# Moving a range's half products into the next range's w_in stage

## The chip, the cores and the metric

One core of a Trainium2 chip runs the whole kernel. The metric is the time of one execution on the device in microseconds; the median of three executions stands for a kernel.

## What is computed

Attention of 12 heads over 8 batches of 448 tokens, then two matrix products with a leaky ReLU between them:

```
attn = softmax(q @ k^T / sqrt(64)) @ v            # q, k, v: 8 x 12 x 448 x 64
x = attn, heads side by side                      # 3584 x 768
h = x @ w_in                                      # 768 x 2048
out = max(0.01 * h, h) @ w_out                    # 2048 x 768
```

The inputs are float32; the kernel's matmuls take bfloat16 and add up in float32.

## The kernel before

**Ranges.** The 3584 tokens are cut into seven ranges, numbered 0 to 6 here (`cuts`): 640, 512, 512, 512, 512, 384 and 512 tokens. From range 1 on, a range i has two stages. `hidden(i)` is its w_in stage: h from x. `second(i)` is its w_out stage: out from h. Attention work for later ranges is put between the matmuls of both.

**The w_in stage** (`hidden`). Matrix products are done in a form with seven products where eight would be plain (sums and differences of blocks are made on VectorE first, so that one product in eight is saved). A group of four 128-wide row blocks of h takes seven products of six matmuls each (L553), 256 token columns wide (192 in range 5). Two groups run in turn, one on the PSUM tiles `banks` (named g in the profile) and one on two of the three `slots` (named sc), and there are two such rounds: 28 products. After a product ScalarE copies it (L565, L573, L577) or VectorE adds it to such a copy (L568, L580, L583); ScalarE writes the leaky ReLU (L542). The sums and differences of h that w_out needs are L525 and L526, those of x that w_in needs are L500 (`mix_x_part`, eight for a range: four over two row blocks and four over one), with six copies L487 at range 2, where the ring that holds x begins anew.

**The w_out stage** (`second`). It walks through two pairs of 128-token blocks (`block_pair(i, c)`, c = 0 and 1). A pair has six products of eight 128x384 matmuls (L682), in turn on the banks b and a; the names `fifth` and `sixth` are the last two of them. Between matmuls, at every `yield`, `second` may put in scores of later attention units (L316, L319; their exponentials are L328 on ScalarE) or `rows`, the weighted sums over v (L340, L347) with their division on VectorE (L968, L969). Scores take all three slots at once, rows and the last part of a unit's scores one. A finished row block is transposed into x by a DMA of the SP queue (L271), q and k of later units into qkT likewise (L280). `keep` (L687) copies a product into the output tile, `join` (L693) adds one, `store` (L399) sends it out; L697 and L703 are differences of h for the pair.

**The half products** (`deep`). What would be the seventh product of both pairs is done together, by the same scheme once more: seven products of four 128x192 matmuls (L644). Each is followed by an addition into an output tile (L645); one more difference of h is L647, and three others are made ahead in `deep_sums` (L620). The seven lie among the fifth and sixth product of the second pair, one after every two matmuls, and use two slots, b and a, alternately; they come in the order b, a, b, a, b, a, b. While they run, only one slot is left for attention work. In the last range, the kernel's end, they stand in the same places; its second pair has its output tiles in the memory of the exponentials (named e).

**What sets the order.** The program fixes the order on each engine; an engine works through its instructions one after the other and waits where a semaphore tells it to. In `second(i)`, the subtractions L500 of the next range are put in one at a time as steps go by, once the planner's clock says that x has arrived; those left over are put at the end of the stage, ahead of `hidden(i + 1)`. In `hidden(i)`, `rows` is called at steps 2, 6, 10, ... as long as rows are owed; two are.

**Tiles.** A slot is one tile of 128 x 2 x 512 float32 numbers. There are three output tiles `o`, five tiles `c` for the copies of w_in products.

```
banks = [ps_g.tile([P, 4 * P], F32, name=f"g{i}") for i in range(2)]
slots = [ps_s.tile([P, 2, 512], F32, name=f"sc{i}") for i in range(3)]
```

Of the kernel before, what the change touches and what calls it, by code (L numbers as in the profile page):

```python
# [16 lines left out]
def kernel(  # L17
# [9 lines left out]
    nc = tc.nc  # L27

    B, H, S, D = q.shape
    DM, DF = moe_w_in.shape  # L30
# [497 lines left out]
    def hidden(i):  # L528

        n = cuts[i + 1] - cuts[i]  # L530
        nh = n // 2
        at = place_of(cuts[i])
        near, far = slice(0, KH), slice(KH, KD)
        one, two = slice(at, at + nh), slice(at + nh, at + n)
        t2, t3, t4 = (x_mix[:, x, :, :nh] for x in range(3))
        hs = h[:, :, spots(i)[0] * P:spots(i)[0] * P + n]
        taken = [next_slot() for _ in range(2)]
        del slots[1:]
        chains = [banks, [x[:, 0] for x in taken]]

        def act(m, cols, x):
            nc.scalar.activation(  # L542
                hs[:, m:m + 2, cols], x.rearrange("p (m t) -> p m t", m=2), AX.Prelu, alpha=0.01
            )

        def group(chain, m):
            b, a = (x[:, :2 * nh] for x in chain)
            left, right = slice(0, nh), slice(nh, n)

            def product(ps, w, x, first=False):  # L550
                for j in range(2):
                    for kk in range(KH):
                        nc.tensor.matmul(  # L553
                            ps[:, j * nh:(j + 1) * nh], w[:, kk, ts(j, P)], x[:, kk],
                            start=(first and j == 0 and kk == 0), stop=(kk == KH - 1), skip_group_check=True,
                        )

            def fresh():
                return c_pool.tile([P, 4 * P], F32, name="c")[:, :2 * nh]

            cl, ch = slice(m * P, (m + 2) * P), slice(FH + m * P, FH + (m + 2) * P)
            s2, s3, s4 = (w_in_mix[:, x, :, cl] for x in range(3))
            product(b, w_in_sb[:, near, cl], xT[:, near, one], first=True)
            c11 = fresh()
            nc.scalar.copy(c11, b)  # L565
            yield
            product(a, w_in_sb[:, far, cl], xT[:, far, one], first=True)
            nc.vector.tensor_add(c11, c11, a)  # L568
            yield
            product(b, s2, t2)  # L570
            act(m, left, c11)
            c12 = fresh()
            nc.scalar.copy(c12, b)  # L573
            yield
            product(a, w_in_sb[:, near, ch], xT[:, near, two], first=True)
            c22 = fresh()
            nc.scalar.copy(c22, a)  # L577
            yield
            product(b, s3, t3)
            nc.vector.tensor_add(c22, c22, b)  # L580
            yield
            product(a, s4, xT[:, far, two])
            nc.vector.tensor_add(c12, c12, a)  # L583
            act(MH + m, right, c22)
            yield
            product(b, w_in_sb[:, far, ch], t4)
            act(m, right, c12)
            act(MH + m, left, b)
            yield

        ready = []
        for r in range(2):
            ms = [4 * r, 4 * r + 2]
            todo = [group(chains[x], ms[x]) for x in range(2)]
            for step in range(7):
                for x in range(2):
                    yield
                    next(todo[x])
                    if step == 2 and ready:
                        mix_h(i, ready.pop(0))  # L600
            for c in chains:
                c.reverse()
            ready += ms
        slots.extend(taken)
        for m in ready:
            mix_h(i, m)
# [16 lines left out]
    def deep(i):  # L623

        one, two = (ts(x[1], P) for x in spots(i)[1])
        lo, hi = slice(MH, MH + QH), slice(MH + QH, MD)
        s3, s1 = h_mix[:, :QH, 0], h_mix[:, QH:, 0]
        t, (t2, t3, t4) = w_mix[:, 2], (deep_mix[:, x] for x in range(3))
        left, right = slice(0, QW), slice(QW, NW)
        o = [kept[i, c] for c in range(2)]  # L630
        end = i + 1 == NR
        taken = [slots.pop(0) for _ in range(2)]
        b, a = (x[:, 0, :QW] for x in taken)
        for ps, first, x, w, c, cols in (
            (b, True, h[:, lo, one], t[:, :QH, left], 0, left),
            (a, True, h[:, hi, one], t[:, QH:, left], 0, left),
            (b, False, s1, t2, 0, right),
            (a, True, h[:, lo, two], t[:, :QH, right], 1, right),
            (b, False, s3, t3, 1, right),
            (a, False, h[:, hi, one], t[:, QH:, right], 0, right),  # L640
            (b, False, h[:, hi, two], t4, 1, left),
        ):
            for m in range(QH):
                nc.tensor.matmul(ps, x[:, m], w[:, m], start=(first and m == 0), stop=(m == QH - 1), skip_group_check=True)  # L644
            nc.vector.tensor_add(o[c][:, cols], o[c][:, cols], ps)  # L645
            if ps is a and first and c == 0:
                nc.vector.tensor_sub(h[:, hi, one], h[:, hi, one], s1)  # L647
            t0 = token(i, spots(i)[1][c][1])
            if ps is a and not first:
                store(o[0], t0, slice(0, NW) if end else slice(0, DM), (nc.sync, nc.scalar if end else nc.sync))  # L650
            if end and c == 1 and ps is b:
                store(o[1], t0, cols, (nc.sync, nc.scalar))
            yield
        if not end:
            store(o[1], token(i, spots(i)[1][1][1]))
        slots.extend(taken)
        for x in taken:
            model["free"][id(x)] = model["now"] + 1.2

    def block_pair(i, c):  # L660

# [30 lines left out]
        def join(o, at, ps):  # L692
            nc.vector.tensor_add(o[:, at], o[:, at], ps[:, :NW])  # L693

        yield
        yield from product(b, h[:, lo, one], w_out_sb[:, lo, left], first=True)
        nc.vector.tensor_sub(h[:, lo, one], h[:, lo, two], h[:, lo, one])  # L697
        short = cuts[i + 1] - cuts[i] < 4 * P
        keep(o1, left, b, idle if c == 0 and short else calm)
        yield  # L700
        yield from product(a, h[:, hi, one], w_out_sb[:, hi, left], first=True)
        join(o1, left, a)
        nc.vector.tensor_sub(h[:, hi, one], h[:, hi, one], h[:, lo, one])  # L703
        yield
        yield from product(b, h[:, lo, one], t2)
        keep(o1, right, b, calm)
        yield
        yield from product(a, h[:, lo, two], t1, first=True)
        keep(o2, right, a, calm)
        yield  # L710

        def fifth():
            yield from product(b, s3, t3)
            if i:
                keep(o2, left, b)
            join(o2, right, b)
            if i:
                if last:
                    store(o1, token(i, x1), left)
                    store(o2, t0, right, (nc.sync, nc.scalar))  # L720
                elif i + 1 == NR:
                    store(o2, t0, right)

        def sixth():
            yield from product(a, h[:, hi, one], w_out_sb[:, hi, right])
            join(o1, right, a)
            store(o1, token(i, x1), right if last else slice(0, DM), (nc.sync, nc.scalar if last else nc.sync))

        if i and c:
            more = deep(i)  # L730
            for _ in fifth():
                yield
                next(more)
                yield
            yield
            for x, _ in enumerate(sixth()):
                yield
                if x != int(last):
                    next(more)
                    yield  # L740
            for _ in more:
                yield
            return
        yield from fifth()
        yield
        sums = deep_sums(i) if i else ()
        for _ in sixth():
            next(sums, None) if i else None
            yield
        if i:  # L750
            return
        yield
# [434 lines left out]
    for i in range(1, NR):  # L1187
        for step, _ in enumerate(hidden(i)):
            advance()
            if owed_t and step == 0:  # L1190
                tail()
            if step % 4 == 2 and rows_done < nxt:
                rows()
            turn_next(i)
        model.update(now=0.0, act=2.3, free={id(x): 0.9 if cuts[i + 1] - cuts[i] == 4 * P and i + 1 < NR else 1.2 for x in slots}, ready={})
        second(i)
# [30 lines left out]
```

## Time and profile before

| | us |
|---|---|
| median of 3 executions | 384.94 (384.92 to 384.98) |
| the profiled execution | 384.23 |
| its span in the profile | 382.4 |
| TensorE busy in it (granted clock 0.997) | 371.8 |
| VectorE, ScalarE, GpSimd busy | 247.6, 257.3, 182.2 |
| TensorE, w_in stage of range 2 (153.2 to 173.6) | 20.16 of 20.40 |
| TensorE, w_out stage of range 2 (173.6 to 201.4) | 27.75 of 27.80 |
| TensorE, end of the kernel (359.0 to 382.4) | 18.39 of 23.40 |

The span runs from the first to the last event of the execution that the profiler recorded. A timeline line names its start, its length, the engine, the line of the kernel, what is written and read, and in brackets how long the engine had been idle and what ended that. A line "x8" stands for eight instructions in a row; their length is that of the row. Matmuls overlap: the next one starts before the one before it has drained, so the distance of two starts says what a product costs.

### The profile page before, as it was taken

The numbers are of one execution on the slowest core, as the hardware profiler recorded it, in microseconds if no ns is written. First come the engines' busy times: TensorE is split into PE (matmuls) and PEld (weight loads), VectorE is DVE, ScalarE is ACT, GpSimd is POOL, SyncE is SP. The second block draws the span as 40 slices with busy tenths as digits, with TensorE's granted clock in tenths as the row PEclk, the third lists the DMA queues.
The fourth block names the chain that finished last, engine by engine and source line by source line (L and its number), as shares of the span: only waits on it lengthen the run. The fifth ranks groups of instructions, "written<-read, shape, count | busy, mean of one in ns | idle before, by whom it ended". The sixth has DMA issues, their size and how long they took to land.

```text
span 382.4 us, 10102 instructions
## 1 busy us (share of the span) xinstructions
PE 371.8 (97%) x4008; PEld 265.4 (69%) x4008; DVE 247.6 (65%) x551; ACT 257.3 (67%) x396; POOL 182.2 (48%) x376
## 2 busy tenths in 40 slices
PE   7999999999999999999999999999999999999994
PEld 3665557766698566886568866688666995678753
DVE  5763858356766867666676675775757774784744
ACT  6988885765768784488764788648786388518620
POOL 8998631987979554840558405685046100000000
PEclk9999999999999999999999999999999999999998
DMA  9999999799999569891499914999238700222032
GB/s 160 200 201 203 178 179 195 94 176 208 143 193 124 82 123 164 183 127 27 97 143 214 144 27 81 153 214 135 41 67 151 175 15 5 74 73 66 1 84 83
DMA packets 99456, 47.85 MB, mean 125 GB/s; under 512 B 63696, under 2 KB 96208, under 8 KB 99408
## 3 DMA queue, kind: packets, MB, share of 16 engines
q0 software_dynamic: 40384, 22.47, 47.6%
q1 hardware_dynamic: 58432, 24.12, 32.4%
q8 instruction: 31, 0.51, 0.5%
q10 hardware_dynamic: 592, 0.61, 0.5%
q14 instruction: 17, 0.14, 0.1%
HBM read 45.61 MB, written 11.01 MB: 148 GB/s over the span
## 4 chain that ended last, share of the span: by engine, by line
PE 89%; DVE 5%; issue 2%; DMA 1%; ACT 1%; POOL 0%; DVEq 0%; POOLq 0%; ACTq 0%
PE g L682 25%; PE g L553 14%; PE sc L553 14%; PE sc L319 7%; PE sc L347 6%; PE g L421 4%; PE sc L316 4%; PE sc L359 3%; PE g L769 3%; PE sc L644 2%; PE g L810 2%; PE sc L340 2%; DMA w_in_mix<-in_q_dram 1%; PE g L359 1%; PE g L298 1%
## 5 line engine op out<-in xcount | busy, mean ns | idle before, releaser
L328 ACT ACTIVATE e<-sc 128x896 bf16<-128x896 f32 (+1 forms) x144 | 123.6, 922 | 33.5 <-PE sc L319 20.4
L682 PE MATMUL g<-w_out_sb,h 128*128 128x384 bf16 x416 | 81.7, 326 | 0.2 <-DVE o L693 0.2
L682 PEld LDWEIGHTS <-h 128*128 128x128 bf16 x528 | 49.1, 98 | 37.5 <-issue 9.6
L186 POOL COPY qkb<-fq 112x512 bf16<-112x512 bf16 x36 | 23.7, 659 | 88.9 <-DMA qkT<-qkb 72.7
L542 ACT ACTIVATE h<-c 128x512 bf16<-128x512 f32 (+1 forms) x72 | 43.5, 611 | 24.8 <-DVE c L568 15.5
L553 PEld LDWEIGHTS <-w_in_sb 128*128 128x128 bf16 x576 | 54.3, 98 | 5.3
L553 PEld LDWEIGHTS <-w_in_mix 128*128 128x128 bf16 x432 | 41.2, 98 | 4.1
L968 DVE RECIPROCAL rec<-sc 112x8 f32<-112x8 f32 x42 | 8.7, 208 | 43.5 <-PE sc L347 22.0
L687 DVE COPY o<-g 128x384 f32<-128x384 f32 x44 | 24.3, 553 | 18.8 <-PE g L682 18.6
L347 PE MATMUL sc<-v,e 128*128 128x65 bf16 x720 | 33.3, 193 | 0.0
L319 PE MATMUL sc<-qkT 64*128 64x448 bf16 (+1 forms) x210 | 32.8, 352 | 0.0
L347 PEld LDWEIGHTS <-e 128*128 128x128 bf16 x720 | 31.2, 98 | 1.3
L969 DVE TENSOR_TENSOR x<-sc,rec 112x512 bf16<-112x512 f32 x42 | 29.0, 691 | 1.5
L553 PE MATMUL sc<-xT,w_in_sb 128*128 128x256 bf16 (+1 forms) x216 | 28.5, 268 | 0.0
L553 PE MATMUL g<-xT,w_in_sb 128*128 128x256 bf16 (+1 forms) x216 | 28.5, 268 | 0.0
L565 ACT COPY c<-g 128x512 f32<-128x512 f32 (+1 forms) x12 | 6.8, 569 | 32.0 <-PE g L553 32.0
L340 PE MATMUL sc<-v,e 128*128 128x130 bf16 x120 | 26.5, 221 | 0.0
L693 DVE TENSOR_TENSOR o<-o,g 128x384 f32<-128x384 f32 x36 | 19.7, 548 | 5.4 <-PE g L682 4.8
L682 PE MATMUL g<-w_mix,hmix 128*128 128x384 bf16 x104 | 23.0, 327 | 0.0
L159 POOL DMA_DIRECT2D fv<-in_v_dram x33 | 20.6, 631 | 4.1 <-POOL v L199 2.4
L159 POOL DMA_DIRECT2D fk<-in_k_dram x33 | 20.9, 645 | 1.4 <-DMA fv<-in_v_dram 1.4
L359 PEld LDWEIGHTS <-e 112*128 112x128 bf16 x432 | 20.0, 98 | 2.1 <-issue 0.7
(144 smaller groups left out, 745.4 us busy)
## 6 DMA issues: line engine op xcount, KB each, us to landing
fq<-in_q_dram POOLq DMA_DIRECT2D x18, 224.0 KB, 6.2
w_in_sb<-in_moe_w_in_dram POOLq DMA_DIRECT2D x4, 768.0 KB, 11.0
w_out_sb<-in_moe_w_out_dram POOLq DMA_DIRECT2D x4, 768.0 KB, 18.8
out_dram<-o SPq DMA_DIRECT2D x7, 336.0 KB, 3.2
out_dram<-o SPq DMA_DIRECT2D x7, 288.0 KB, 5.0
fk<-in_k_dram POOLq DMA_DIRECT2D x15, 128.0 KB, 6.3
fv<-in_v_dram POOLq DMA_DIRECT2D x15, 128.0 KB, 5.6
out_dram<-o SPq DMA_DIRECT2D x7, 240.0 KB, 3.4
```

What stands on the lines that cost most here:

```text
L159: nc.gpsimd.dma_start(out=t[p, :n, :, :so].rearrange("p u h so d -> p (u h) (so d)"), in_=(q, k, v)[x][b, hs, keys].rearrange("h (p so) d ...
L186: by(t[:SC, x].rearrange("p so h d -> p h so d"), f)
L319: nc.tensor.matmul(ps[:, j, :S].rearrange("p (so s) -> p so s", so=NSC), t[p, 1, c], t[p, 0, :, :SC], start=True, stop=True,)
L328: nc.scalar.activation(e[:, :, c, :], ps[:n, :, :S], AX.Exp, scale=scale)
L340: nc.tensor.matmul(ps, e[:, EM + qc * SC:EM + qc * SC + P], vt[:, 2 * KC:].rearrange("p j d -> p (j d)"), start=True, stop=False, skip_gro ...
L347: nc.tensor.matmul(ps[:, j * (D + 1):(j + 1) * (D + 1)], e[:, at:at + P], vt[:, j * KC + c], start=False, stop=(c == KC - 1), skip_group_c ...
L359: nc.tensor.matmul(ps[:, qc, :], t[:SC, at:at + P], vt[:, c], start=(c == 0), stop=(c == NSC - 1),)
L542: nc.scalar.activation(hs[:, m:m + 2, cols], x.rearrange("p (m t) -> p m t", m=2), AX.Prelu, alpha=0.01)
L553: nc.tensor.matmul(ps[:, j * nh:(j + 1) * nh], w[:, kk, ts(j, P)], x[:, kk], start=(first and j == 0 and kk == 0), stop=(kk == KH - 1), sk ...
L682: nc.tensor.matmul(ps[:, cols], x[:, m], w[:, m], start=(first and m == 0), stop=(m == MH - 1), skip_group_check=True,)
L687: by(o[:, at], ps[:, :NW])
L969: nc.vector.tensor_mul(x, ps[:, :, :, :D], rec.to_broadcast([SC, 2, 2 * NP, D]))
```

## The change

From range 2 on, `hidden(i)` runs the half products of range i - 1: one behind each of its first seven products. (Range 0 has none; those of range 6 have no w_in stage after them.) `deep` takes one slot and uses the tile's two halves as b and a. The w_out stage of ranges 1 to 5 ends with the fifth and sixth product alone. In `hidden(i)` from range 2 on, rows are called from step 10 on, no longer at steps 2 and 6.

In the last range the half products follow the second pair's second, third and fourth product, one after every four matmuls, and the seventh after the fourth product. Since its second output tile has no sum yet then, two of them are copied there by ScalarE (L649) instead of added, and the fifth product is added on its left side too. The sixth product is split into two halves of 192 columns, the first on bank a, the second on half a slot; the right part of the fourth product in bank a that is no longer added to is added by itself (L714), and each half is stored by itself. One store of the first output tile comes earlier.

```diff
@@ -589,6 +589,7 @@
             yield
 
         ready = []
+        more = deep(i - 1) if i > 1 else None
         for r in range(2):
             ms = [4 * r, 4 * r + 2]
             todo = [group(chains[x], ms[x]) for x in range(2)]
@@ -596,6 +597,8 @@
                 for x in range(2):
                     yield
                     next(todo[x])
+                    if i > 1:
+                        next(more, None)
                     if step == 2 and ready:
                         mix_h(i, ready.pop(0))
             for c in chains:
@@ -629,8 +632,8 @@
         left, right = slice(0, QW), slice(QW, NW)
         o = [kept[i, c] for c in range(2)]
         end = i + 1 == NR
-        taken = [slots.pop(0) for _ in range(2)]
-        b, a = (x[:, 0, :QW] for x in taken)
+        slot = slots.pop(0)
+        b, a = (slot[:, x, :QW] for x in range(2))
         for ps, first, x, w, c, cols in (
             (b, True, h[:, lo, one], t[:, :QH, left], 0, left),
             (a, True, h[:, hi, one], t[:, QH:, left], 0, left),
@@ -642,20 +645,18 @@
         ):
             for m in range(QH):
                 nc.tensor.matmul(ps, x[:, m], w[:, m], start=(first and m == 0), stop=(m == QH - 1), skip_group_check=True)
-            nc.vector.tensor_add(o[c][:, cols], o[c][:, cols], ps)
+            if end and c and (ps is a or cols is left):
+                nc.scalar.copy(o[c][:, cols], ps)
+            else:
+                nc.vector.tensor_add(o[c][:, cols], o[c][:, cols], ps)
             if ps is a and first and c == 0:
                 nc.vector.tensor_sub(h[:, hi, one], h[:, hi, one], s1)
-            t0 = token(i, spots(i)[1][c][1])
             if ps is a and not first:
-                store(o[0], t0, slice(0, NW) if end else slice(0, DM), (nc.sync, nc.scalar if end else nc.sync))
-            if end and c == 1 and ps is b:
-                store(o[1], t0, cols, (nc.sync, nc.scalar))
+                store(o[0], token(i, spots(i)[1][0][1]), slice(0, NW) if end else slice(0, DM))
             yield
         if not end:
             store(o[1], token(i, spots(i)[1][1][1]))
-        slots.extend(taken)
-        for x in taken:
-            model["free"][id(x)] = model["now"] + 1.2
+        slots.append(slot)
 
     def block_pair(i, c):
 
@@ -692,61 +693,73 @@
         def join(o, at, ps):
             nc.vector.tensor_add(o[:, at], o[:, at], ps[:, :NW])
 
-        yield
-        yield from product(b, h[:, lo, one], w_out_sb[:, lo, left], first=True)
-        nc.vector.tensor_sub(h[:, lo, one], h[:, lo, two], h[:, lo, one])
-        short = cuts[i + 1] - cuts[i] < 4 * P
-        keep(o1, left, b, idle if c == 0 and short else calm)
-        yield
-        yield from product(a, h[:, hi, one], w_out_sb[:, hi, left], first=True)
-        join(o1, left, a)
-        nc.vector.tensor_sub(h[:, hi, one], h[:, hi, one], h[:, lo, one])
-        yield
-        yield from product(b, h[:, lo, one], t2)
-        keep(o1, right, b, calm)
-        yield
-        yield from product(a, h[:, lo, two], t1, first=True)
-        keep(o2, right, a, calm)
-        yield
-
-        def fifth():
+        def early():
+            yield from product(b, h[:, lo, one], w_out_sb[:, lo, left], first=True)
+            nc.vector.tensor_sub(h[:, lo, one], h[:, lo, two], h[:, lo, one])
+            short = cuts[i + 1] - cuts[i] < 4 * P
+            keep(o1, left, b, idle if c == 0 and short else calm)
+            yield
+            yield from product(a, h[:, hi, one], w_out_sb[:, hi, left], first=True)
+            join(o1, left, a)
+            if last:
+                store(o1, token(i, x1), left)
+            nc.vector.tensor_sub(h[:, hi, one], h[:, hi, one], h[:, lo, one])
+            yield
+            yield from product(b, h[:, lo, one], t2)
+            keep(o1, right, b, calm)
+            yield
+            yield from product(a, h[:, lo, two], t1, first=True)
+            keep(o2, right, a, calm)
+            if last:
+                nc.vector.tensor_add(o1[:, NW + QW:], o1[:, NW + QW:], a[:, QW:NW])
+            yield
+
+        def late():
             yield from product(b, s3, t3)
-            if i:
+            if i and not last:
                 keep(o2, left, b)
             join(o2, right, b)
-            if i:
-                if last:
-                    store(o1, token(i, x1), left)
-                    store(o2, t0, right, (nc.sync, nc.scalar))
-                elif i + 1 == NR:
-                    store(o2, t0, right)
-
-        def sixth():
-            yield from product(a, h[:, hi, one], w_out_sb[:, hi, right])
-            join(o1, right, a)
-            store(o1, token(i, x1), right if last else slice(0, DM), (nc.sync, nc.scalar if last else nc.sync))
-
-        if i and c:
+            if last:
+                store(o2, t0, right, (nc.sync, nc.scalar))
+                join(o2, left, b)
+                store(o2, t0, left, (nc.sync, nc.scalar))
+            elif i + 1 == NR:
+                store(o2, t0, right)
+            yield
+            if not last:
+                yield from product(a, h[:, hi, one], w_out_sb[:, hi, right])
+                join(o1, right, a)
+                store(o1, token(i, x1))
+                return
+            for x, ps in enumerate((a, slots[0][:, 0])):
+                cols = ts(x, QW)
+                yield from product(ps, h[:, hi, one], w_out_sb[:, hi, right][:, :, cols], first=bool(x), cols=cols)
+                at = slice(NW + x * QW, NW + (x + 1) * QW)
+                nc.vector.tensor_add(o1[:, at], o1[:, at], ps[:, cols])
+                store(o1, token(i, x1), at, (nc.sync, nc.scalar))
+                if not x:
+                    yield
+
+        yield
+        if last:
             more = deep(i)
-            for _ in fifth():
+            for x, _ in enumerate(early()):
                 yield
-                next(more)
-                yield
-            yield
-            for x, _ in enumerate(sixth()):
-                yield
-                if x != int(last):
-                    next(more)
+                if x > 3 and x % 2:
+                    next(more, None)
                     yield
             for _ in more:
                 yield
+            yield from late()
             return
-        yield from fifth()
-        yield
-        sums = deep_sums(i) if i else ()
-        for _ in sixth():
-            next(sums, None) if i else None
-            yield
+        yield from early()
+        sums = deep_sums(i) if i and not c else iter(())
+        for x, _ in enumerate(late()):
+            if x > 3:
+                next(sums, None)
+            yield
+        for _ in sums:
+            pass
         if i:
             return
         yield
@@ -1189,7 +1202,7 @@
             advance()
             if owed_t and step == 0:
                 tail()
-            if step % 4 == 2 and rows_done < nxt:
+            if step % 4 == 2 and rows_done < nxt and (step > 8 or i == 1):
                 rows()
             turn_next(i)
         model.update(now=0.0, act=2.3, free={id(x): 0.9 if cuts[i + 1] - cuts[i] == 4 * P and i + 1 < NR else 1.2 for x in slots}, ready={})
```

## The prediction

> **What bounds the kernel now.** I read the page first, then the timeline of TensorE alone to list its gaps, then the timeline of all engines where w_out of one range ends and w_in of the next begins, then the last 15 us.
>
> ```profile
> PE 371.8 (97%) x4008; PEld 265.4 (69%) x4008; DVE 247.6 (65%) x551; ACT 257.3 (67%) x396; POOL 182.2 (48%) x376
> ```
>
> TensorE is busy for 371.8 of 382.4 us. The missing 10.6 us are 1.20 before the first matmul, some 3.2 in gaps of 0.13 to 0.44 up to 58 us, 1.07 + 0.12 at the ends of w_out stages, 0.23 in the last stage, and 4.8 behind the last matmul. From 58 us to 377 us TensorE rarely waits, so any wait put there is paid in full, and the most that can be won in the middle is about 1.4 us. The 1.07 us are these two waits in range 1:
>
> ```profile
> 152.57 0.49 PE L644 MATMUL sc<-w_mix,h 128*128 128x192 bf16 x4 [0.69 <-DVE o L645]
> ...
> 153.44 0.49 PE L644 MATMUL sc<-deep_mix,h 128*128 128x192 bf16 x4 [0.38 <-DVE o L645]
> ```
>
> A half product waits there for VectorE to have added up the one two places earlier. In range 2 the same place shows 0.06 us:
>
> ```profile
> 196.94 0.49 PE L682 MATMUL g<-w_mix,hmix 128*128 128x384 bf16 x2
> 197.14 0.56 DVE L687 COPY o<-g 128x384 f32<-128x384 f32 x1 [1.71 <-PE g L682]
> 197.61 0.41 DVE L500 TENSOR_TENSOR x_mix<-xT 128x512 bf16<-128x512 bf16 x1
> ...
> 201.41 0.49 PE L644 MATMUL sc<-w_mix,h 128*128 128x192 bf16 x4
> 201.73 0.29 DVE L500 TENSOR_TENSOR x_mix<-xT 128x256 bf16<-128x256 bf16 x1
> ...
> 202.19 0.82 PE L553 MATMUL g<-xT,w_in_sb 128*128 128x256 bf16 x6
> 202.84 0.82 PE L553 MATMUL sc<-xT,w_in_sb 128*128 128x256 bf16 x6
> ```
>
> The reader is to see three things. A product of six w_in matmuls takes 0.655 us (202.19 to 202.84). VectorE starts 0.20 us after TensorE has passed on (the fifth product begins at 196.94, the copy of the fourth at 197.14). And the token subtractions of the next range (L500) stand between the additions, in a queue that works in order.
>
> **The prices.** Eight 128x384 matmuls take 1.30 us (368.64 to 369.94), four 128x192 ones 0.33. On VectorE, counted to the next start: copy and addition of 384 columns 0.47 and 0.46, addition of 192 columns (L645) 0.27, or 0.35 to its end; subtraction L500 of 512 columns 0.33, or 0.46 where it needs the one just before (0.42 + 0.04); of 256 columns 0.33 in a dependent row (342.01, 342.33, 342.66, 342.99); addition L568 0.60; L653, the old L647, 0.33. TensorE goes on 0.06 after the end of an addition (152.17 + 0.34 to 152.57).
>
> **The moved half products.** Their 5 x 28 matmuls and 35 additions are the same work in another place: 0 on TensorE as long as no wait comes. In the changed kernel's order of instructions one comes. Both halves now lie in one tile, and each half product waits for the addition of the half product just before it, where it waited for the one two before. One round is 0.20 + 0.35 + 0.06 = 0.61 us, and the cover is one w_in product, 0.655: enough, if VectorE is free at once. It is not. All subtractions L500 of the next range now stand ahead of the first of these additions, because w_out's two last products are 2.3 us (7 x 0.33) shorter and nothing separates them from the stage's end.
>
> Range 2 to 3, counted from the fifth product's start F. VectorE: copy to 0.67, two L500 to 1.43, copy of the fifth product from 1.50, addition to 2.43 (its end 2.52), two L500 to 3.22, addition of the sixth product to 3.67, four small L500 at 3.67, 4.00, 4.32, 4.65, first half addition 4.85 to 5.20. TensorE: two products to 2.60, w_in, half product, w_in to 2.60 + 0.655 + 0.33 + 0.655 = 4.24; the second half product may start at 5.26. **Wait 1.02 us**. Two places on, an L568 of 0.60 stands ahead of a half addition: 0.20 + 0.60 + 0.35 + 0.06 against 0.33 + 0.655, **0.23** more. After that the rounds fit.
>
> The five boundaries by the same steps:
> Range 1 to 2 has six copies L487 of 0.23 in that queue too: w_in starts 0.30 late, the second half product 2.07, then 0.23: 2.60. From this 1.07 of waits goes away: +1.53.
> Range 2 to 3: the last transpose was issued at 194.73 and took 6.2 to land, 200.93, while VectorE asks for it at 200.61: 1.02 + 0.32 + 0.23 - 0.06 = +1.51.
> Range 3 to 4: +1.19.
> Range 4 to 5 has 192 token columns: L500 shorter (0.35 and 0.25 each), but a w_in product covers only 0.50 of the 0.61: wait 1.09, then 0.24 and four times 0.12: +1.81.
> Range 5 to 6: all eight L500 stand behind the sixth product: four big ones from 3.26 to 4.97, four small ones to 6.15, half addition to 6.50: wait 6.56 - 4.24 = 2.32, then 0.23: +2.55.
> GpSimd's copies slow an L500 that they meet: 0.69 for 0.42 at 152.43. They fall on the queue again in three of these places: 3 x 0.23 = +0.7, my estimate from that row; 0 and 1.5 are its ends.
> Sum **+9.3**. Its lower bound has no GpSimd (-0.7) and no gaps between dependent subtractions (some 0.3 at each boundary): +7. Its upper one has double the GpSimd cost and transposes that land 1 us later in three places: +13.
>
> The Trainium skill (PSUM — Partial Sum Buffer, Terms) forbids two engines in one bank of 2 KiB at the same time; the two halves lie in two banks, so by this rule the second half product need not wait for the first addition, and the third would be the one to wait. By that rule this part costs +2.6 instead of +9.3 (rival B).
>
> **Rows moved from products 2 and 6 to 10 and 14.** The same matmuls; the SP and GpSimd queues keep their order. Cover: the next transposes into qkT waited for scores at 177.91 and GpSimd stood idle for 13.89 us there, so 5 us later costs 0; without that cover it would be up to 5 x 5 us. The two stores of half sums wait for additions in mid-stage, with only these transposes behind them.
>
> **The last range.** Six half products go among products 2 to 4 of the second pair, one per four matmuls (0.65 us of cover), the sixth product becomes 16 matmuls of 192 (0.02 more). From the second product at 368.64: the second half addition stands behind L693 and the long L703 (0.60), end 371.89, wait **0.70**; the last half product waits for an addition behind a new one (L714) that needs ScalarE's copy of the fourth product: product ends 374.90, copy to 375.58, L714 to 375.91, addition to 376.26, wait **1.09**; 0.04 in between. Matmuls end at 376.65 + 1.30 + 0.66 + 0.66 = 379.27, before at 377.45: +1.82. Then addition to 379.82. Each queue issues a store every 0.42 to 0.46 us, and its fourth of the tail starts near 380.3:
>
> ```profile
> 378.33 0.32 ACTq L399 DMA_DIRECT2D out_dram<-o  x1
> 378.75 0.40 ACTq L399 DMA_DIRECT2D out_dram<-e  x1
> ```
>
> against 378.75 here, **+1.6**. Bounds: -0.4 (no wait, shorter last piece) and +2.2.
>
> **Sum.** 9.3 + 1.6 = +10.9. The profiled execution took 384.23, 1.83 more than its span; so 393.3 of span and 395.1. The median shown, 384.94, lies 0.71 above that execution: **395.8**.
>
> **Rivals.**
> A, faster: VectorE's backlog is gone when the stage starts, so each round of 0.61 fits under 0.655 and no half product waits. Then the old waits go (1.07 + 0.12), and the tail ends 0.4 earlier: 383.4. For it: VectorE is busy only 65%, and is freed of 2.4 us (7 x 0.35) just before. Against: the order puts L500 first, up to 2.9 us of it behind the last product. It decides from the point where the first half addition starts before w_in + 1.4 us.
> B: the two halves are waited for apart. The first wait shrinks by 0.33 + 0.655 at each boundary (0.33 + 0.50 between 4 and 5) and L568's falls away: +0.3, +0.3, 0, +0.3, +1.3 in order, GpSimd 0.4, tail -0.2: +2.4, 387.3. Against: the waits in the program name the addition just before.
> C: TensorE's clock falls in the long waits. After the last matmul (377.61) the granted clock is 1.00 up to 380.00, and then:
>
> ```profile
> 380.00:380.50 0.50, 0.00 (x0) 0.00 (x0) 0.00 (x0) 0.00 (x0) 0.00 (x0) 0.74 0.68 217
> 380.50:381.00 0.50, 0.00 (x0) 0.00 (x0) 0.00 (x0) 0.00 (x0) 0.00 (x0) 0.50 0.01 2
> ```
>
> It falls to half about 2.6 us after the last matmul. The two longest waits here, 2.07 and 2.32, minus 0.17 in which the last matmul drains, come to within 0.7 and 0.45. If both pass it and half speed lasts as long as the idling that brought it (2.6 us), each costs 1.3: +2.6, 398.4. The Trainium skill (TensorE: Matmul & The Clock Gate, Part 1) names about 3.4 us of idling before half speed; the 2.6 of the row is shorter and decides, and by the skill's figure this rival would be out.
>
> **How the numbers follow.** Forecast 0.83, A 0.05, B 0.04, C 0.06, rest (no change: the waits fall where nothing follows) 0.02. The forecast's own range is 393 to 398; A and most of B are left out, C is taken in: 391.5 to 398.5. Chances, with 0.2% (0.8 us) as what a measurement of this kernel can tell from no change: faster 0.05, same 0.02, slower 0.93.
>
> **What would show it.** In the timeline of each boundary from 150 us on, the second half product (now L647) with a wait of 1 to 2.3 us on L651, with L500 just before that addition on VectorE; the fourth with 0.2; between 4 and 5 small waits at nearly all; in the last range waits of 0.7 and 1.1, the latter behind L714; busy matmul time unchanged near 372; and a last store on ScalarE's queue 3.6 us before the end. It is wrong if the second half product starts without a wait, if its wait is put to a DMA, or if waits appear at L682's successor (L683) or in the scores.

## Result and profile after

The changed kernel takes 396.33 us, median of 4 executions (395.38 to 398.74), beside 384.93 for the kernel before (384.69 to 384.98, 4 executions): ratio 1.0307, 95% interval 1.0256 to 1.0358. It is slower. The profiled execution took 395.45 with a span of 393.6, which is 11.2 us longer than before.

The page of the changed kernel, busy times and the shares of the chain that ended last:

```profile
PE 374.2 (95%) x4016; PEld 266.5 (68%) x4016; DVE 252.2 (64%) x551; ACT 259.3 (66%) x398; POOL 183.2 (47%) x376
...
PE 84%; DVE 9%; issue 2%; DMA 2%; ACT 1%; POOL 0%; POOLq 0%; DVEq 0%; ACTq 0%
```

TensorE is busy 2.4 us more than before for the same work: 1.1 of them in the opening, where both kernels run the same instructions, and 1.3 behind it, where the last matmul ahead of a wait counts as busy while it drains. The rest of the 11.2 us is idle. The view of waits says for whom (waited for, total us, times, longest):

```profile
PE sc L647 <- DVE o L651: 10.2, 9, 2.5
```

Nine waits of half products (L647) for the addition (L651) make 10.2 us. In the timeline of the changed kernel (start, length, engine, line; in brackets the idle time and what ended it), the boundary of ranges 1 and 2, that of 5 and 6, and the last range:

```profile
151.67 0.82 PE L553 MATMUL sc<-xT,w_in_sb 128*128 128x256 bf16 x6
151.81 0.42 DVE L500 TENSOR_TENSOR x_mix<-xT 128x512 bf16<-128x512 bf16 x1
152.26 0.61 DVE L500 TENSOR_TENSOR x_mix<-xT,x_mix 128x512 bf16<-128x512 bf16 x1
152.79 0.24 DVE L487 COPY xT<-xT 128x192 bf16<-128x192 bf16 x1
...
154.21 0.47 DVE L500 TENSOR_TENSOR x_mix<-xT,x_mix 128x256 bf16<-128x256 bf16 x1
154.60 0.34 DVE L651 TENSOR_TENSOR o<-o,sc 128x192 f32<-128x192 f32 x1
155.00 0.49 PE L647 MATMUL sc<-w_mix,h 128*128 128x192 bf16 x4 [2.51 <-DVE o L651]
...
348.55 0.29 DVE L500 TENSOR_TENSOR x_mix<-xT,x_mix 128x256 bf16<-128x256 bf16 x1
348.75 0.35 DVE L651 TENSOR_TENSOR o<-o,sc 128x192 f32<-128x192 f32 x1
349.15 0.49 PE L647 MATMUL sc<-w_mix,h 128*128 128x192 bf16 x4 [2.16 <-DVE o L651]
...
381.31 0.49 PE L647 MATMUL sc<-deep_mix,hmix 128*128 128x192 bf16 x4 [0.60 <-DVE o L651]
...
385.62 0.49 PE L647 MATMUL sc<-deep_mix,h 128*128 128x192 bf16 x4 [0.86 <-DVE o L651]
```

At 151.67 TensorE issues its second w_in product and then has nothing it may do until 155.00: the first half product is long done, but its addition waits at the end of VectorE's queue, behind subtractions for products that TensorE has not reached. At 349.15 it is the same.

**Where the 11.2 us are.** The ends of a range's w_in stage (the end of its last L553 row in TensorE's timeline) cut the span into comparable pieces, each with the same matmuls in both kernels:

| piece, ending with | before, us | after, us | difference |
|---|---|---|---|
| w_in of range 1 (opening) | 124.80 | 125.19 | +0.39 |
| w_in of range 2 | 49.48 | 51.27 | +1.79 |
| w_in of range 3 | 48.42 | 49.94 | +1.52 |
| w_in of range 4 | 48.43 | 50.02 | +1.59 |
| w_in of range 5 | 43.79 | 45.36 | +1.57 |
| w_in of range 6 | 44.40 | 46.83 | +2.43 |
| last matmul | 18.29 | 20.12 | +1.83 |
| end of the span | 4.8 | 4.9 | +0.1 |

The opening runs the same instructions in both kernels; its 0.39 is a difference between two executions.

### The profile page after: what moved, and what is told of

Its sections match the earlier page's. It is cut to its first block, busy times and chain, and to the rows that moved or that the text cites. A ratio compares the mean times of both kernels' runs of the same rounds, so it can differ in the third digit from the quotient of the medians.

```text
span 393.6 us, 10116 instructions
## 1 busy us (share of the span) xinstructions
PE 374.2 (95%) x4016; PEld 266.5 (68%) x4016; DVE 252.2 (64%) x551; ACT 259.3 (66%) x398; POOL 183.2 (47%) x376
## 4 chain that ended last, share of the span: by engine, by line
PE 84%; DVE 9%; issue 2%; DMA 2%; ACT 1%; POOL 0%; POOLq 0%; DVEq 0%; ACTq 0%
PE g L683 24%; PE sc L553 12%; PE g L553 12%; PE sc L319 7%; PE sc L347 6%; PE g L421 4%; PE sc L316 4%; PE sc L647 3%; PE sc L359 3%; PE g L782 3%; PE g L823 2%; DVE x_mix L500 2%; PE sc L340 2%; DMA w_in_mix<-in_k_dram 2%; DVE o L651 1%
## 5 line engine op out<-in xcount | busy, mean ns | idle before, releaser
L683 PE MATMUL g<-w_out_sb,h 128*128 128x384 bf16 (+1 forms) x416 | 79.5, 325 | 0.2 <-DVE o L694 0.2
L186 POOL COPY qkb<-fq 112x512 bf16<-112x512 bf16 x36 | 24.2, 672 | 75.6 <-DMA qkT<-qkb 60.6
L553 PEld LDWEIGHTS <-w_in_sb 128*128 128x128 bf16 x576 | 54.4, 98 | 5.8 <-issue 0.3
L553 PEld LDWEIGHTS <-w_in_mix 128*128 128x128 bf16 x432 | 40.9, 98 | 3.8
L197 POOL COPY v<-fv 128x384 bf16<-128x384 bf16 x30 | 15.6, 522 | 37.1 <-PE sc L347 23.1
L553 PE MATMUL g<-xT,w_in_sb 128*128 128x256 bf16 (+1 forms) x216 | 28.5, 268 | 0.1
L553 PE MATMUL sc<-xT,w_in_sb 128*128 128x256 bf16 (+1 forms) x216 | 28.5, 268 | 0.0
L651 DVE TENSOR_TENSOR o<-o,sc 128x192 f32<-128x192 f32 x39 | 13.7, 350 | 13.0 <-PE sc L647 13.0
L316 PE MATMUL sc<-qkT 64*128 64x448 bf16 x144 | 19.8, 361 | 1.7 <-DVE qkT L302 0.8
L683 PE MATMUL g<-w_mix,h 128*128 128x384 bf16 x112 | 21.3, 326 | 0.0
```

The lines of the kernel that those rows point to most:

```text
L186: by(t[:SC, x].rearrange("p so h d -> p h so d"), f)
L316: nc.tensor.matmul(ps[:, j, :S], t[p, S + c * SC:S + c * SC + P], t[p, :S], start=True, stop=True)
L553: nc.tensor.matmul(ps[:, j * nh:(j + 1) * nh], w[:, kk, ts(j, P)], x[:, kk], start=(first and j == 0 and kk == 0), stop=(kk == KH - 1), sk ...
L683: nc.tensor.matmul(ps[:, cols], x[:, m], w[:, m], start=(first and m == 0), stop=(m == MH - 1), skip_group_check=True,)
```

## Experiments

Most of these kernels start from the changed one and hold both versions of the edited functions. `HID` lists the ranges whose w_in stage takes the half products of the range before (2 to 6 in the change), `NEW_LAST` says whether the last range is the changed one. Two more lines stand ahead, so L647 and L651 are L649 and L653 there, L553 is L555, L500 is L502 and L487 is L489. Columns 2 to 7 of this table are the pieces of the table above, from the profiled execution of each, less those of the kernel before, in us:

| | to w_in 2 | 3 | 4 | 5 | 6 | last matmul | median, us | ratio (95%) |
|---|---|---|---|---|---|---|---|---|
| the change | +1.79 | +1.52 | +1.59 | +1.57 | +2.43 | +1.83 | 396.33 | 1.031 (1.026 to 1.036) |
| e1 | +3.85 | +1.45 | +1.61 | +1.58 | +2.43 | +0.01 | 395.23 | 1.027 (1.024 to 1.030) |
| e2 | +0.12 | 0.00 | +0.01 | -0.01 | +0.01 | +1.83 | 386.63 | 1.005 (1.003 to 1.007) |
| e3 | -0.53 | -0.02 | +0.07 | +0.67 | +0.11 | +1.84 | 386.44 | 1.005 (1.003 to 1.006) |
| e4 | +1.30 | +1.88 | +2.07 | +1.78 | +2.03 | +1.69 | 394.24 | 1.025 (1.023 to 1.028) |
| e5 | +4.88 | +0.01 | 0.00 | 0.00 | +2.42 | +0.01 | 391.58 | 1.017 (1.016 to 1.019) |
| e6 | 0.00 | +1.81 | +0.98 | +1.57 | 0.00 | 0.00 | 389.78 | 1.015 (1.011 to 1.018) |
| e7 | +0.30 | -0.12 | -0.31 | -0.04 | +0.72 | +0.01 | 385.61 | 1.003 (1.002 to 1.005) |
| e8 | +0.54 | -0.15 | -0.12 | -0.10 | +0.72 | +0.01 | 385.59 | 1.002 (1.000 to 1.004) |
| e9 | +1.25 | +0.75 | +0.77 | +1.13 | +1.90 | +0.01 | 391.62 | 1.017 (1.014 to 1.020) |
| e10 | +0.59 | -0.02 | -0.19 | -0.17 | +1.89 | +0.01 | 386.50 | 1.004 (1.002 to 1.005) |
| e11 | +0.15 | -0.33 | -0.09 | -0.09 | 0.00 | 0.00 | 384.67 | 1.000 (0.998 to 1.001) |

The kernel before, run beside them, had medians of 384.64 to 384.83. Each experiment's expectation follows as it was written ahead of its run.

**e1 and e2: the two parts apart.**

```diff
+    HID = (2, 3, 4, 5, 6)
+    NEW_LAST = False
```

> The moved half products of ranges 1 to 5 as in the change, the last range as before. My theory (the second half product waits for its addition behind the next range's subtractions): the five boundaries alone cost 9.0 us (the late starts in the two profiles: 3.2, 1.9, 2.0, 1.8, 2.6 after, 2.5 in all before), so some 394 us, with waits of 2.5, 1.3, 1.4, 0.9 and 2.2 us at the same places. Rival (the last range is the larger part): under 389 us. If the clock falls in the two long waits in some executions, these are some 2 to 3 us longer, at a mean clock of 0.99.

```diff
+    HID = ()
+    NEW_LAST = True
```

> Only the last range's part of the change; ranges 1 to 5 as before. My theory: two waits of 0.7 and 1.0 us, behind the long subtraction of h and behind the new addition L714, cost 1.6 to 1.9 us: 386.5 to 386.8 us, with all executions within 0.3 us of each other. Rival (the split sixth product shortens the tail by more than the waits cost): 384.5 or less.

The last range alone costs +1.83 to its last matmul, and its two waits (0.60 and 0.86) are those of the changed kernel; e2's executions spread over 0.85 us, not the 0.3 expected. The ranges alone cost the rest at the same five places. e1 came out 1.2 us above its expectation, all at one place, 1 to 2. The windows of e1 there (stretch, length, busy time of PE, PEld, DVE, ACT and POOL, then TensorE's granted clock) say why:

```profile
155.50:156.00 0.50, 0.50 (x7) 0.48 (x7) 0.04 (x1) 0.00 (x0) 0.50 (x1) 1.00 0.00 0
156.00:156.50 0.50, 0.50 (x6) 0.36 (x4) 0.50 (x2) 0.00 (x0) 0.50 (x2) 0.61 0.00 0
156.50:157.00 0.50, 0.50 (x5) 0.42 (x3) 0.15 (x2) 0.00 (x0) 0.50 (x2) 0.50 0.31 37
...
159.00:159.50 0.50, 0.50 (x5) 0.42 (x4) 0.50 (x1) 0.00 (x0) 0.00 (x0) 0.50 1.02 96
159.50:160.00 0.50, 0.50 (x6) 0.45 (x5) 0.37 (x2) 0.00 (x0) 0.00 (x0) 0.97 1.30 163
```

The clock is half from about 156.11 (0.61 of a half-us window is 0.11 at full and 0.39 at half speed) to 159.53, after a wait of 2.96 us that had ended at 155.43. Half speed for 3.42 us of work costs 1.7. The other 0.36 by which this piece exceeds that of the change (+3.85 beside +1.79) goes with a longer wait, 2.96 us instead of 2.51: the copy L489 of the ring's end ahead of it, for one, took 0.51 us and not 0.24.

**e3: the subtractions taken away.** The subtractions of x that are left over at a stage's end are not done in ranges 2 to 6.

```diff
+        if i + 1 in HID:
+            return
         for todo in x_sums:
             for _ in todo:
                 pass
```

> The change, with those subtractions of x (and the last wrap copy) left out that stand at the end of a w_out stage behind the sixth product's addition, so that the products that read them get old numbers. My theory: without this backlog on VectorE the second half product doesn't wait at all in the 256-column ranges; what stays is 0.3 us at the fourth half product of each range, 0.7 between ranges 4 and 5, and the last range's 1.8: 386.5 us. Rival (one tile for both halves is the cost by itself, or the transposes are late): 392 us or more.

The view of waits of this kernel, beside 10.2 in nine with them:

```profile
PE sc L649 <- DVE o L653: 1.9, 4, 0.9
```

The five boundaries together cost +0.3 instead of +8.9; the last range, which has no such subtractions, keeps its +1.84. The half products start late by some 2.8 us in all there, where the old places were late by 2.45 (counted from the start that the cover would allow, as explained further down). So the new places, the one tile and the moved rows together cost next to nothing more than the old places did, where VectorE is free. Only 4 to 5 keeps +0.67: its w_in products of 192 columns take 0.50 us, and a round of 0.61 does not fit under that.

**e4: one tile in the old places.** The kernel before, with both halves in one of its two slots and nothing moved:

```diff
-        b, a = (x[:, 0, :QW] for x in taken)
+        b, a = (taken[0][:, x, :QW] for x in range(2))
```

> The kernel before, with only one thing of the change: both halves of the half products lie in one slot's tile, at their old places among the fifth and sixth product. The second slot stays unused. My theory: each half product now waits for the addition just before it; a round is 0.61 us and its cover 0.33 (two 128x384 matmuls), nothing ahead of the last one, so 0.28 x 4 + 0.61 = 1.7 us or more in each of six ranges, where 2.5 us in all were there before: 393 to 400 us. Rival (the two halves are separate banks, and are waited for apart): 384.9, no change.

This alone costs +10.75 to the last matmul. The whole change costs +10.73 there; that the two agree is chance, since the waits stand in other places. TensorE in its w_out stage of range 2 (its half product is L794, the addition L795):

```profile
200.05 0.49 PE L794 MATMUL sc<-w_mix,h 128*128 128x192 bf16 x4 [0.27 <-DVE o L795]
200.37 0.49 PE L832 MATMUL g<-w_mix,hmix 128*128 128x384 bf16 x2
...
203.45 0.49 PE L794 MATMUL sc<-deep_mix,hmix 128*128 128x192 bf16 x4 [0.34 <-DVE o L795]
...
205.44 0.49 PE L794 MATMUL sc<-deep_mix,h 128*128 128x192 bf16 x4 [0.57 <-DVE o L795]
```

Two matmuls of 384 columns (200.37 and on) are 0.33 us of cover for a round of 0.61. This settles that the halves of one tile are not waited for apart: were they, nothing here would have changed. No run has two tiles in the new places, so how much of the change's waits a second tile would have taken away is not measured.

**e5 and e6: the long waits and the short ones apart.**

```diff
+    HID = (2, 6)
+    NEW_LAST = False
```

> Half products moved at the boundaries 1 to 2 and 5 to 6 alone (the two with the longest waits), last range as before. My theory: 1.8 + 2.4 = 4.2 us, 389.1. If TensorE's clock falls in waits of over 2 us in some executions, the executions differ by 1 to 3 us and the long ones show a mean clock below 0.997. Rival (the scatter has another cause): all within 0.5 us.

```diff
+    HID = (3, 4, 5)
+    NEW_LAST = False
```

> Half products moved at the boundaries 2 to 3, 3 to 4 and 4 to 5 alone. My theory: 1.5 + 1.6 + 1.6 = 4.7 us, 389.6, and as no wait is over 1.6 us all executions lie within 0.5 us of each other. Rival (scatter has another cause than the long waits): they differ by 1 us or more.

e6 met its 389.6 in the median (389.78), but not in the spread. One of its four executions took 392.74 at a clock of 0.990, though the traced one has no wait over 1.6 us; the other three differ by 1.2 us at clocks of 0.997 and more, where 0.5 was expected. That is what its rival foretold: not all of the scatter comes from long waits. e5 took 391.58, 2.5 over its 389.1, and all four of its executions show a clock of 0.988 to 0.992. In the traced one the clock fell in the wait at 1 to 2 (TensorE's timeline, then the windows):

```profile
155.60 0.80 PE L649 MATMUL sc<-w_mix,h 128*128 128x192 bf16 x4 [3.11 <-DVE o L653]
156.19 1.48 PE L555 MATMUL g<-xT,w_in_sb 128*128 128x256 bf16 x6
157.47 0.84 PE L649 MATMUL sc<-deep_mix,hmix 128*128 128x192 bf16 x4
```

```profile
154.00:154.50 0.50, 0.00 (x0) 0.00 (x0) 0.47 (x2) 0.00 (x0) 0.48 (x1) 0.99 0.68 182
154.50:156.00 1.50, 0.40 (x3) 0.38 (x3) 1.01 (x3) 0.00 (x0) 1.44 (x5) 0.50 0.53 176
...
161.00:162.00 1.00, 1.00 (x11) 0.83 (x10) 0.15 (x1) 0.48 (x1) 0.00 (x0) 0.84 1.25 156
```

A w_in product takes 1.28 (156.19 to 157.47) instead of 0.655. Half speed lasts from 154.49 to 161.32, 6.83 us, of which 5.72 lie after the wait's end: 2.86 us of loss. Without them the +4.88 is +2.02.

**e7 and e8: more room between half products.** They come behind every second w_in product from the second one on (in range 6 from the fourth), rows from step 18 on; in e8 range 2 begins at the fourth as well, and rows are called from step 22 on.

```diff
+    HID = (2, 3, 4, 5, 6)
+    NEW_LAST = False
...
-                    if i > 1:
+                    if i in HID and 14 * r + 2 * step + x >= {6: 3}.get(i, 1) and (14 * r + 2 * step + x - {6: 3}.get(i, 1)) % 2 == 0:
                         next(more, None)
```

> Half products in the next w_in stage as in the change, but one behind every second w_in product (from the second on; from the fourth in the last range), rows from step 18 on, and the last range as before. My theory: a round of 0.61 us, or 1.2 with an L568 ahead, now has 1.64 us of cover and the backlog of 2.3 us is done before the second one, so no half product waits; all 2.5 us of late starts of the kernel before at these places go: 382.5 us, at most 383.5. Rival (half products in w_in cost time by themselves, or the later rows and stores do): 384.9 or more.

> The change in ranges 1 to 5 with the half products behind every second w_in product, as in the run before, but beginning at the fourth w_in product at the boundaries 1 to 2 and 5 to 6 instead of the second; the last range as before the change. Theory (a half product waits only because VectorE works off the token subtractions first; two products later it is through with them): the 0.66 us wait of the second half product after range 1 and the 0.53 after range 5 go, the 0.49 of a w_in product at 152.6 stays because it waits for the copies of the ring's end and not for a half product. About 1.0 us less than every second product from the second on: 384.6 (383.8 to 385.4), no difference from the kernel before. Rival (what is left there is a wait of the one tile, which moves along with the half products): 385.6 as before, with waits of 0.5 or more at the new places.

e7 missed its 382.5 by 3 us. The three middle boundaries do gain, 0.47 in all, but the two others lose 1.02, with half products that wait 0.66 and 0.53. At 1 to 2 a w_in product now waits for VectorE itself, for a copy of the ring's end (L489):

```profile
153.09 0.60 PE L555 MATMUL g<-xT,w_in_sb 128*128 128x256 bf16 x4 [0.49 <-DVE xT L489]
...
155.00 0.49 PE L649 MATMUL sc<-w_mix,h 128*128 128x192 bf16 x4 [0.66 <-DVE o L653]
```

e8's expectation was wrong in one thing: at 5 to 6 e7 already began at the fourth product, so only 1 to 2 is tested. There the half product's wait shrinks from 0.66 to 0.30 instead of going, but the w_in product meets the copy 0.33 earlier, the copy itself (0.51 us long instead of 0.23) ends 0.28 later, and the wait for it is 1.08 (+0.54 instead of +0.30). The two kernels take the same time, where e8 was to win 1.0.

**e9 and e10: the additions first.** The changed order of half products (e9) and that of every second product (e10), with the leftover subtractions two at a time behind the first three w_in products and the rest behind the fourth.

```diff
+        rest = (y for todo in (left_sums.pop() if left_sums else ()) for y in todo)
...
                         next(more, None)
+                        for _ in range(2 if 2 * step + x < 3 else 20):
+                            next(rest, None)
...
+        if i + 1 in HID:
+            for todo, y in zip(x_sums, (0, 2)):
+                while i == 1 and y not in wrapped:
+                    next(todo)
+            left_sums.append(x_sums)
+            return
```

> The change in ranges 1 to 5 with the half products at the change's own places (behind each of the first seven w_in products), the last range as before the change; alone the order on VectorE differs: the leftover subtractions L500 of x are no longer all ahead of the first half addition, but two of them behind each of the first three w_in products and the rest behind the fourth (at the boundary 1 to 2 the copies of the ring's end still come first). Nothing is left out. Theory (the wait is VectorE's queue): the first half addition starts when its half product ends, a round of two subtractions and an addition takes about 1.0 us against a cover of 0.985, and the waits of 2.67, 1.45, 1.53, 1.09 and 2.33 us of the second half product become 0 to 0.6 each at the second to fifth half product; ranges together 1 to 3 us over the kernel before, 385 to 388. Rival (the wait comes from the one tile at any order, or from w_in products that now wait for their sums): 392 or more, with waits of 1 us or more at the second half product or at the fifth w_in product.

> Both of these together: half products behind every second w_in product from the second on, the leftover subtractions two at a time behind the first three w_in products and the rest behind the fourth, the last range as before the change. Theory: the round of a half product has 1.64 us of cover and no more than 1.1 us of VectorE ahead of it, so no half product waits over 0.2 us; the 0.49 of a w_in product behind the copies of the ring's end stays. The visible waits ahead of the change (1.07 and 0.12) are gone as well: about 0.5 us under the kernel before, 384.2 (383.5 to 385.0), at most 0.2% faster. Rival: 385.6 as without the reordering.

Both came out above what the theory gave, e9 by 3.6 us over its upper end, e10 by 1.5. The wait of the second half product is gone or down to 0.22, but VectorE's work is not. In e9 the wait comes back at the fourth half product (1.33, 0.66, 0.65, 0.54 and 0.85 at the five boundaries). In e10 it comes back at w_in products, 1.00 at 1 to 2 and 1.91 at 5 to 6 (its L500 is L506, its w_in product L559):

```profile
343.47 0.35 DVE L661 TENSOR_TENSOR o<-o,sc 128x192 f32<-128x192 f32 x1
343.73 0.42 DVE L663 TENSOR_TENSOR h<-h,hmix 128x512 bf16<-128x512 bf16 x1
344.07 0.28 DVE L506 TENSOR_TENSOR x_mix<-xT 128x256 bf16<-128x256 bf16 x1
344.39 0.29 DVE L506 TENSOR_TENSOR x_mix<-xT,x_mix 128x256 bf16<-128x256 bf16 x1
344.41 0.60 PE L559 MATMUL g<-x_mix,w_in_mix 128*128 128x256 bf16 x4 [1.91 <-DVE x_mix L506]
```

Behind the last w_out product VectorE has some 3 us of subtractions to do at 5 to 6, and TensorE's fifth product needs the results of seven of the eight (the one begun at 344.07 released it). Additions put ahead of them delay them; additions put behind them delay the half products.

**e11: only where VectorE is free.**

```diff
+    HID = (3, 4, 5)
+    NEW_LAST = False
...
+                    if i in HID and 14 * r + 2 * step + x >= 1 and (14 * r + 2 * step + x - 1) % 2 == 0:
                         next(more, None)
```

> Half products behind every second w_in product, from the second on, at the three boundaries 2 to 3, 3 to 4 and 4 to 5 alone; at 1 to 2, at 5 to 6 and in the last range everything as before the change. From the ends of the w_in stages in the profile of the kernel with every second product at all five: range by range +0.30, -0.12, -0.31, -0.04 and +0.72 us against the kernel before; the three in the middle together -0.47. Theory (a half product costs nothing more where VectorE is free in time, and the short waits of the old places go away): 0.5 us less than before in the span from the opening's end on, 384.3 to 384.6, which this measurement hardly tells from no change. Rival (GpSimd's copies and the held slot cost it elsewhere): 385 or more, with a wait of scores or of L500's readers at a new place.

The three pieces gain 0.51 in the profile; the median of 12 executions, 384.67, cannot be told from 384.71 before. No version here beats the kernel before by more than that.

## Why the prediction was right, point by point

**The mechanism held.** The second half product waits for L651 behind L500 at all five boundaries, the fourth by 0.08 to 0.25, and L649 and L714 bring the last range's two waits. e3 shows the cause, e2 the last range alone. Size by size:

- **Boundaries.** Predicted +1.53, +1.51, +1.19, +1.81 and +2.55, and +0.7 of GpSimd over all: +9.3. Measured +1.79, +1.52, +1.59, +1.57, +2.43: +8.9. Three terms were mis-sized, and that the errors nearly cancel is luck.
- **The waits that go away** were put at 1.19, the gaps seen before. A gap shows only once the last matmul has drained, 0.16 us (a w_in row is 0.82 long, the next starts after 0.655), so a matmul that is late by less shows none. Counted from the start that the cover would allow, those of before were late by 1.39, 0.34, 0.36, 0.18 and 0.18: 2.45. The new waits had been counted from that start, the old ones from the gap, so the sum came out 1.26 too high here.
- **GpSimd.** At 1 to 2 three L500 took 0.61, 0.58 and 0.47 for 0.42, 0.29 and 0.29; at 2 to 3 one took 0.67; at 3 to 4 two took 0.60 and 0.47. That makes 1.5 us, the upper end and not the 0.7 that I took (by the row that I went by, 0.69 for 0.42, one meeting costs 0.27 and not 0.23). L653 was slowed too, 0.67 for 0.42 at 2 to 3 and 3 to 4, and the fourth half product was 0.41 late there beside 0.28 at 1 to 2 and 5 to 6.
- **The late transpose** of 2 to 3, put at 0.32, did not come: no L500 there waits for a DMA. A copy of GpSimd took its place, so that +1.51 met +1.52 for another reason than the one given:

```profile
202.85 0.29 DVE L500 TENSOR_TENSOR x_mix<-xT 128x256 bf16<-128x256 bf16 x1
203.17 0.29 DVE L500 TENSOR_TENSOR xT<-xT 128x256 bf16<-128x256 bf16 x1
203.50 0.29 DVE L500 TENSOR_TENSOR x_mix<-xT 128x256 bf16<-128x256 bf16 x1
203.74 0.61 POOL L186 COPY qkb<-fq 112x512 bf16<-112x512 bf16 x1 [4.33 <-DMA qkT<-qkb]
203.83 0.67 DVE L500 TENSOR_TENSOR x_mix<-xT,x_mix 128x256 bf16<-128x256 bf16 x1
```

- **4 to 5**: the late starts of its seven half products add up to 1.76, predicted 1.81; the 0.18 of before go off that.
- **Last range.** Its matmuls end +1.83 later (predicted +1.82). The shorter last piece was to win 0.2 behind them and won nothing: 4.9 us from the last matmul to the end of the span, 4.8 before.
- **Rows moved** cost nothing that shows: e3 has them moved and its five boundaries come to +0.3.
- **The profiled execution** was predicted at 395.1 and took 395.45, of which 0.39 is the opening. The median was predicted from it by adding the 0.71 by which the median before lay higher. It lies 0.9 higher, but, going by the clocks, for another reason: rival C. That 395.8 came within 0.6 of 396.33 is thus luck in part.

**Rivals.** A (VectorE is free in time) fell with the first wait. B (halves waited for apart) fell in e4: by the rule of the Trainium skill's page "PSUM — Partial Sum Buffer" (Terms) the two halves may be used at once, since they lie in two banks, but the waits in this program are made by tile. C, given 0.06, does happen, in some executions: the profiled one had the clock at 1.00 up to its last matmul, and the two long ones were at 0.994 (397.21) and 0.991 (398.74), 1.8 and 3.3 above it. That is near one and two times the 1.7 us that the trace of e1 shows for one fall; these two were not traced. What failed in C is its condition: it isn't a length of idling that the wait must pass (e5, below).

## What to carry to other kernels

Moving matmuls under a cover moves their readers too: count what stands ahead of those readers in their engine's queue at the new place, in time, not the engine's share of busy time over the span. Where that engine is in arrears, another order only chooses which matmul waits, and two buffers in one tile take away the one round of slack that hid the arrears (e4 shows that in the old places). And count lateness, not gaps: a wait shorter than the drain of the last matmul is paid but not seen.

## What the hardware showed that was not expected

**The clock's fall is not set by the wait's length alone.** After the same last matmul (drained near 152.5) it fell at 154.49 in e5, 2.0 us later and in the wait; at 156.11 in e1, when TensorE had worked again for 0.7 us; and not at all in the changed kernel's profiled execution (wait 2.51). So 2.0 us of idling were enough once and 2.51 were not another time. It stayed at half for 6.83 and 3.42 us, two to one. The kernel before has single executions of this kind too (387.77 at 0.988); what sets them off is open. The Trainium skill ("TensorE: Matmul & The Clock Gate", Part 1) describes a free-running window of some 3.4 us in which activity is watched. Both durations agree with that; its "idle window" does not, if it means a window without work, since the wait in e5 was 2.0 us old when the clock fell.

**GpSimd holds VectorE up until its own copy ends.** In the changed kernel L500 at 152.26 ended at 152.87, 0.28 after the end of GpSimd's copy L190 (151.85 for 0.74); those at 153.59 and 154.21 ended 0.14 after L186 and L190.

```profile
151.85 0.74 POOL L190 COPY qkb<-fk 128x384 bf16<-128x384 bf16 x1
152.26 0.61 DVE L500 TENSOR_TENSOR x_mix<-xT,x_mix 128x512 bf16<-128x512 bf16 x1
...
153.39 0.64 POOL L186 COPY qkb<-fq 112x512 bf16<-112x512 bf16 x1
153.59 0.58 DVE L500 TENSOR_TENSOR x_mix<-xT 128x256 bf16<-128x256 bf16 x1
```

The Trainium skill ("SBUF — State Buffer", section "SBUF: two separate sides") has a port pair that the two share and that the first to start holds for its whole instruction while the other is blocked; these rows agree, up to the 0.14 to 0.28 by which the blocked one ends later. The prediction had an estimate of 0.7 us for it from one row; by such a rule it would have had to be worked out copy by copy.
